# Last inverse transform of a spectral filter beside attention: constants as weights, the spectrum in two float32r parts as 256 moving columns, a turned output, and a new list of batches

## The chip, the cores and the metric

One core of a Trainium2 chip runs the whole kernel. Its engines are TensorE (PE, with the weight loads PEld), VectorE (DVE), ScalarE (ACT), GpSimd (POOL) and SyncE (SP, which issues most DMAs). The metric is the device time of one execution in microseconds; lower is better. The time before is the median of three runs.

## What is computed

Two independent layers read their own inputs; the results stand side by side in the last axis. The first is attention with 16 query heads of width 28 that share one key head and one value head, over 2048 rows. The second is a filter in the spectrum: a real two-dimensional Fourier transform over 2048 x 448, a product with complex weights, and the inverse transform.

```python
def _A_ref(x, wq, wk, wv, wo):
    q = (x @ wq).reshape(B, S, H, Dh).transpose(0, 2, 1, 3)
    k = x @ wk
    v = x @ wv
    scores = jnp.einsum("bhqd,bkd->bhqk", q, k) * (Dh ** -0.5)
    p = _softmax(scores, axis=-1)
    o = jnp.einsum("bhqk,bkd->bhqd", p, v)
    return o.transpose(0, 2, 1, 3).reshape(B, S, H * Dh) @ wo

def _B_ref(x, w_r, w_i):
    X = jnp.fft.rfft2(x, axes=(-2, -1))
    X = X * (w_r + 1j * w_i)
    return jnp.fft.irfft2(X, s=(S, D), axes=(-2, -1))
```

with B = 1, S = 2048, D = 448, H = 16, Dh = 28.

## The kernel before

**Attention.** After the projections (lines up to some 400) the work goes in 256 steps: 4 blocks of 512 queries (c) x 4 groups of 4 heads (g) x 16 blocks of 128 keys (kc). In a step PE makes four score tiles of 128 x 512 (line 867, float32r; here "a score"), ACT takes the exponential of each out of PSUM (line 811), and PE multiplies with the values (`flush`, line 822, four float32 products of 32 columns side by side). After 16 steps the sum of a (c, g) is turned (line 826) and normalised (`norm`, `divide`); the output projection is done in units of (c, k, g) (`wo_unit`, matmuls on line 731).

**The filter.** It is cut into matrix products, spread between the scores. Part one (`fft1_*`) transforms along D and partly along S, and writes `t1` to DRAM; it is nearly done before the 256 steps, and only the last unit, `fft1_b(7)`, stands among them. Part two (`fft2_a`, `fft2_b`, 16 units each) finishes the transform along S, multiplies with the weights, begins the inverse and writes `t2` to DRAM. Its operands are already kept as two float32r parts: a high part, which is a rounded copy, and a low part, which is the difference; `mm3` (line 555) adds three products: high by high, low by high, high by low. Part three reads `t2` back (`fft3_load`, eight loads q, each with its own constants `fi`):

- `fft3_a(q, e)` finishes the inverse along S for the even (e = 0) or odd (e = 1) frequencies of D: four float32 matmuls of 128 columns into one PSUM bank (line 655), and one DVE copy to `z` (line 658).
- `fft3_b(q, v)` does the inverse along D for 128 rows of the result: four float32 matmuls (line 669) in which a 128-column piece of `z` is the weights and the constants `cs3` are the 113 moving columns. DVE copies two of the products out (line 673), adds and subtracts (lines 674 and 675); POOL makes the final sums and differences (lines 679 and 680), and SP stores them (line 682).

**The list.** `PLAN` holds one string for each batch of steps; PE's order is written out by it. In a string, `-` is a score whose exponential ACT takes straight from PSUM; `k` is a score of the batch's last step that DVE copies to SBUF first (line 873) and ACT takes from there in one operation of 1024 columns (line 890); `e` is one of the last step that ACT takes at once. `F` is the last unit of part one, `A` and `B` a unit of `fft2_a` and `fft2_b`, `W` a unit of the output projection, `Z` a unit of part three in the order a, a, b, b for each q. X stands for WWWW and Y for ZZ. `spread(n, units, lazy, start, rest)` makes a string of n steps and sets the units at even distances: unit j at (4n - 4)(j + start)/(units + rest), less 0.4. The scores of a batch come first, its value products at the end; the last step's products wait for the next batch. `where` holds the step at which each unit falls, and with `at(step, ...)` loads and splits are hung on it: `fft3_load(q)` eight steps ahead of its first Z, but not before the last B.

**Banks and queues.** PSUM has eight banks. One holds the running sum of the value products; scores and units share the others through `take` and `give`, which choose the bank that a small model of the clocks of PE, ACT and DVE says is free first. A bank is free for PE again when the last operation that reads it is done. DVE, too, works in an order that is written out: what must follow a unit at once is put there, and other work (`put`) waits in two queues, from which `passed` takes operations as the modelled time goes on; `need(key)` takes them until the one named is out. SP and POOL issue DMAs in the order of the program and wait in it, so a transfer that waits holds up all behind it. `behind` sets an order of issue alone.

**Buffers.** The pool `fp` has tags that several tiles share, one after another: `wi` and `cst` hold `z` in part three, `pwr` holds `y1`, `pwi` holds `yo`, `cs` holds first `cs1` and later `cs3`, and `b2` holds the loaded `c2`.

Of the kernel before, what the change touches and what calls it, by code (L numbers as in the profile page):

```python
# [10 lines left out]
F32 = mybir.dt.float32  # L11
F32R = mybir.dt.float32r
# [3 lines left out]
ALU = mybir.AluOpType  # L16
AX = mybir.AxisListType
# [3 lines left out]
S, D, H = 2048, 448, 16  # L21
# [16 lines left out]
def spread(n, units, lazy=4, start=0.9, rest=0.85):  # L38

    m = 4 * n - 4  # L40
    out = [(float(i), "-") for i in range(m)]
    out += [(j + 0.5 if j < lazy else m + 0.1 * j, "k" if j < lazy else "e") for j in range(4)]
    out += [(m * (j + start) / (len(units) + rest) - 0.4, u) for j, u in enumerate(units)]
    return "".join(k for _, k in sorted(out)).replace("X", "WWWW").replace("Y", "ZZ")


PLAN = ["eeeeF", "eeee"] + 4 * [spread(2, "", 0)]
FIVE, SIX = spread(5, "BA"), {u: spread(6, u) for u in ("X", "Y", "BAX", "XBB")}
PLAN += [spread(5, "A", 4, 1.6), spread(5, "A")] + 11 * [FIVE] + [SIX["X"], FIVE, SIX["X"], SIX["BAX"], FIVE]
PLAN += [SIX["XBB"], spread(5, "")]  # L50
PLAN += 4 * [SIX["Y"]] + 4 * [SIX["X"]] + 7 * [SIX["Y"]] + 4 * [SIX["X"]] + 3 * [SIX["Y"]] + 2 * [spread(5, "Y")]


WARM = 10, 10
# [3 lines left out]
def kernel(ctx: ExitStack, tc: tile.TileContext, t: dict):  # L58
    nc = tc.nc
    mm = nc.tensor.matmul  # L60
# [3 lines left out]
    fp = ctx.enter_context(tc.tile_pool(name="fp", bufs=2))  # L64
# [29 lines left out]
    fc, xb, ff = {}, {}, {}  # L94
# [147 lines left out]
    with tc.tile_pool(name="w1", bufs=1) as w1:  # L242
# [37 lines left out]
        with tc.tile_pool(name="x1", bufs=2) as x1:  # L280
# [124 lines left out]
            for c in range(1, NC):  # L405
                for g in range(NG):
# [83 lines left out]
    d, f, a, b, e, c = free  # L490
# [34 lines left out]
    def passed(work):  # L525

        clock["pe"] += work
        while any(queue) and clock["dve"] <= clock["pe"]:
            pop()
        clock["dve"] = max(clock["dve"], clock["pe"] - 512)  # L530

    def at_once(work=640, engine="dve"):
        clock[engine] = max(clock[engine], clock["pe"] + 200) + work

    begun = []
# [41 lines left out]
    pr, cst = {}, {}  # L577
# [52 lines left out]


    def fft3_consts():
        fc["cs3"] = fp.tile([113, 4, 113], F32, name="cs3", tag="cs", bufs=1)
        behind(nc.gpsimd.dma_start(fc["cs3"], t["cs3"]), begun[-1])

    t2v = t2.rearrange("(r l n) h f -> r l h n f", r=2, l=2)
    c2 = {}
# [12 lines left out]
    def fft3_a(q, e):  # L650
        w, o0 = ((113, 0), (112, 113))[e]
        bank = take()
        pz = bank.rearrange("p (j n) -> p j n", j=4)
        for j in range(4):
            mm(pz[:w, j], c2["c", q][:, j, o0:o0 + w], c2["F", q][:, j], start=True, stop=True)  # L655
        passed(872)
        z = c2["z", q, e] = fp.tile([113, 2, 4, 64], F32, name=f"z{e}", tag=("wi", "cst")[e])
        nc.vector.tensor_copy(z[:w], pz[:w].rearrange("p j (r n) -> p r j n", r=2))
        at_once()
        give(bank)  # L660

    def fft3_b(q, v):
        ze, zo = c2["z", q, 0], c2["z", q, 1]
        cs3 = fc["cs3"]
        js = slice(2 * v, 2 * v + 2)
        bank = take()
        py = bank[:, :452].rearrange("p (k n) -> p k n", k=4)
        for k, (z, w, r) in enumerate(((ze, 113, 0), (zo, 112, 0), (zo, 112, 1), (ze, 113, 1))):
            mm(py[:, k], z[:w, r, js], cs3[:w, k], start=True, stop=True)  # L669
        passed(888)  # L670
        y1 = fp.tile([128, 2, 2, 113], F32, name="y1", tag="pwr")
        m = fp.tile([128, 2, 113], F32, name="m", tag="us", bufs=1)
        nc.vector.tensor_copy(m, py[:, 2:4])
        nc.vector.tensor_tensor(y1[:, :, 0], py[:, 0:2], m, op=ALU.add)
        nc.vector.tensor_tensor(y1[:, :, 1], py[:, 0:2], m, op=ALU.subtract)  # L675
        at_once(1100)
        give(bank)
        yo = fp.tile([128, 4, 113], F32, name="yo", tag="pwi")
        nc.gpsimd.tensor_tensor(yo[:, 0:2], y1[:, 0], y1[:, 1], op=ALU.add)  # L679
        nc.gpsimd.tensor_tensor(yo[:, 2:4], y1[:, 0], y1[:, 1], op=ALU.subtract)  # L680
        r0 = (2 * q + v) * 128
        nc.sync.dma_start(t["ob"][r0:r0 + 128], yo)


    oh, ol, osb = {}, {}, {}
# [76 lines left out]
    def at(step, f, *a):  # L762
        later.setdefault(max(step, 0), []).append((f, a))
# [3 lines left out]
            "B": [(fft2_b, u) for u in range(16)],  # L767
            "W": [(wo_unit, c, k, g) for c in range(NC - 1) for k in range(4) for g in range(NG)],
            "Z": [(f, q, e) for q in range(8) for f in (fft3_a, fft3_b) for e in range(2)]}
    todo = {k: deque(v) for k, v in todo.items()}  # L770

    where, total = {}, 0
    for tokens in PLAN:
        n, x = sum(k in "-ke" for k in tokens) // 4, 0
# [5 lines left out]
    fft2_consts()  # L780
    at(1, fft2_load, 0)
    at(where["A"][0] - 1, fft2_split, 0)
    at(14, fft3_consts)
    for u, step in enumerate(where["A"]):
        if u % 2 == 0 and u < 14:
            at(step - 1, fft2_load, u // 2 + 1)
# [59 lines left out]
    begin = 0  # L846
    for tokens in PLAN:
        n = sum(k in "-ke" for k in tokens) // 4
# [4 lines left out]
        new, lazy, x = [], [], {"-": 0, "k": 0}  # L853
        keep = [pp.tile([128, 2, CW], F32, name="k", bufs=4) for _ in range(2)]
        for k in tokens:
# [5 lines left out]
            i, h = divmod(x[kind], 4)  # L861
# [3 lines left out]
            c, g, kc = steps[i if kind == "-" else n - 1]  # L865
# [25 lines left out]
        else:  # L891
            for h in lazy:
                p = keep[h // 2][:, h % 2]
# [8 lines left out]
    c = NC - 1  # L902
# [30 lines left out]
    a, b, d = spare  # L933
    rv = nc.values_load(bits.bitcast(I32)[0:1, 0:1])
    with tc.If(rv > int(np.float32(BOUND).view(np.int32))), tc.tile_pool(name="g1", bufs=1) as g1:
# [12 lines left out]
        with tc.For_i(0, 64, 1) as n:  # L948
# [3 lines left out]
            for i in range(4):  # L952
                r = slice(32 * i, 32 * i + 32)
# [10 lines left out]
        w = g1.tile([128, NG, D], F32, name="w")  # L964
        nc.sync.dma_start(w, t["wo"][:, 0:NG])
        qv = qraw.rearrange("p g (c q) -> p c g q", q=CW)
        oa = t["oa"].rearrange("(n p) d -> n p d", p=128)
        with tc.For_i(0, NC, 1) as nq:
            y = g1.tile([128, 4, D], F32, name="y")
            nc.vector.memset(y, 0.0)  # L970
            with tc.For_i(0, NG, 1) as ng:
# [5 lines left out]
                for i in range(4):  # L977
                    r = slice(32 * i, 32 * i + 32)
                    acc = g1.tile([32, CW], F32, name="acc")
                    nc.vector.memset(acc, 0.0)  # L980
                    with tc.For_i(0, 16, 1) as nk:
# [5 lines left out]
                        p = g1.tile([128, CW], F32, name="pe")  # L987
# [3 lines left out]
                    z = g1.tile([32, CW], F32, name="z")  # L991
# [100 lines left out]
def _gather(oa, ob):  # L1092
    out = np.empty((1, S, 2 * D), np.float32)
    out[0, :, :D] = oa
    y = ob.reshape(32, 64, 4, 113).transpose(1, 0, 2, 3).reshape(S, 4, 113)
    d = np.arange(113)
    b = out[0, :, D:]
    b[:, d] = y[:, 0]
    b[:, D - d[1:]] = y[:, 1, 1:]
    b[:, D // 2 - d[:112]] = y[:, 2, :112]  # L1100
    b[:, D // 2 + d[1:112]] = y[:, 3, 1:112]
    return out


_OUTS = {"oa": (S, D), "ob": (S, 4, 113)}


# [14 lines left out]
```

## Time and profile before

| | before |
|---|---|
| median of 3 runs | 646.97 us (646.79 to 647.3) |
| profiled execution | 646.39 us, its span 644.5 us |
| ACT | 552.6 us busy, 86% |
| DVE | 370.6 us busy, 58% |
| POOL | 79.9 us busy, 12% |
| matmuls of fft3_a (line 655) | 128 instructions, first at 320.0 us, last at 611.3 us |
| matmuls of fft3_b (line 669) | 128 instructions, first at 333.0 us, last at 622.4 us |
| granted clock of PE | 0.999 |

The profile is of one execution. Times are in microseconds from the start of the span, "ns" where it says so. A row of the timeline gives the start, the length, engine, source line, operation, tiles written and read, shape, and how many equal instructions in a row were merged; in brackets stands idle time before it and what ended it. The length of merged matmuls runs to the modelled end of the last, so the pace of PE is read from start to start. A float32 matmul shows as two instructions, a float32r matmul as one. A row of grouped instructions gives the count, then busy time and the mean of one, then the idle time before them. In the rows of a line's own view, three figures with slashes are the shortest, median and longest duration in ns. A window's row has the busy times of PE, PEld, DVE, ACT and POOL in that order.

### The profile page before, as it was taken

To read this page: it belongs to the slowest core of one execution; us is meant where nothing else is said; L and a number is where in the kernel's file an instruction comes from. 1 tells how busy PE (TensorE), PEld (TensorE's weight loads), DVE (VectorE), ACT (ScalarE), POOL (GpSimd) and SP (SyncE) were. 2 spreads that over 40 slices of the span, in tenths; PEclk is the share of its full clock that TensorE was granted. 3 is DMA by queue.
4 is the path that set the end of the run, shared out by engine and by line. 5 is a ranking of instruction groups with operands and counts; after the bars stand their busy time and mean duration, and the time that the engine had idled before them with its cause. 6 is when DMAs were issued, how large, how long until landed. Compare 5 with 4: busy or idle time off the path is not lost.

```text
span 644.5 us, 12021 instructions
## 1 busy us (share of the span) xinstructions
PE 639.0 (99%) x4470; PEld 381.5 (59%) x4470; DVE 370.6 (58%) x683; ACT 552.6 (86%) x1011; POOL 79.9 (12%) x150
## 2 busy tenths in 40 slices
PE   9999999999999999999999999999999999999997
PEld 7877555555555556655555566556655566556655
DVE  5999538989997937465543523354545342363531
ACT  5655999999998989988999898998999898998891
POOL 3022301001211110001020300011031100010110
PEclk9999999999999999999999999999999999999999
DMA  8766953446734522213242403014241403131001
GB/s 275 263 182 167 269 135 101 115 99 155 189 87 112 142 59 72 55 59 103 56 114 59 114 16 80 29 41 122 52 122 42 103 15 80 44 92 20 30 31 60
DMA packets 36113, 63.83 MB, mean 99 GB/s; under 512 B 7905, under 2 KB 23922, under 8 KB 35084
## 3 DMA queue, kind: packets, MB, share of 16 engines
q1 hardware_dynamic: 30832, 49.60, 27.7%
q0 software_dynamic: 4640, 12.48, 7.5%
q10 hardware_dynamic: 576, 0.92, 0.4%
q8 instruction: 36, 0.59, 0.4%
q14 instruction: 29, 0.24, 0.1%
HBM read 30.04 MB, written 14.75 MB: 69 GB/s over the span
## 4 chain that ended last, share of the span: by engine, by line
PE 96%; DMA 1%; DVE 1%; SPq 1%; issue 0%; ACT 0%; ACTq 0%; DVEq 0%
PE s L867 30%; PE s L822 23%; PE po L822 7%; PE s L342 6%; PE sx L867 5%; PE sx L822 4%; PE po L867 4%; PE s L731 4%; PE s L140 2%; PE s L655 2%; PE s L669 2%; PE po L731 1%; PE pbb L159 1%; DMA qa<-qa 1%; PE s L290 1%; PE s L558 1%
## 5 line engine op out<-in xcount | busy, mean ns | idle before, releaser
L811 ACT ACTIVATE p<-s 128x512 f32<-128x512 f32 x632 | 340.1, 627 | 37.1 <-PE s L867 31.4
L867 PE MATMUL s<-qa,ka 128*128 128x512 f32 x782 | 238.0, 407 | 0.3 <-DMA qa<-qa 0.2
L867 PEld LDWEIGHTS s<-qa,ka 128*128 128x128 f32 x782 | 143.2, 188 | 73.7 <-issue 33.1
L873 DVE COPY k<-s 128x512 f32<-128x512 f32 x131 | 84.1, 683 | 125.4 <-PE s L867 125.4
L822 PE MATMUL s<-p,vs 128*32 128x512 f32 x1112 | 132.3, 595 | 0.0
L890 ACT ACTIVATE k<-k 128x1024 f32<-128x1024 f32 x88 | 90.3, 1108 | 0.0
L822 PEld LDWEIGHTS s<-p,vs 128*32 128x32 f32 x1112 | 33.5, 109 | 72.6 <-issue 70.9
L811 ACT ACTIVATE p<-sx 128x512 f32<-128x512 f32 x109 | 68.3, 626 | 7.0 <-PE sx L867 6.4
L811 ACT ACTIVATE p<-po 128x512 f32<-128x512 f32 x83 | 52.8, 636 | 4.8 <-PE po L867 2.3
L867 PE MATMUL sx<-qa,ka 128*128 128x512 f32 x130 | 53.2, 409 | 0.0
L867 PE MATMUL po<-qa,ka 128*128 128x512 f32 x112 | 45.2, 403 | 0.0
L822 PE MATMUL s<-k,vs 128*32 128x512 f32 x296 | 38.7, 594 | 0.0
L822 PE MATMUL po<-p,vs 128*32 128x512 f32 x328 | 38.5, 594 | 0.0
L695 POOL DMA_DIRECT2D ol<-ol x36 | 18.0, 508 | 130.1 <-DVE ol L718 65.4
L679 POOL TENSOR_TENSOR yo<-y 128x226 f32<-128x226 f32 x16 | 9.5, 596 | 190.7 <-DVE y L675 98.1
L867 PEld LDWEIGHTS sx<-qa,ka 128*128 128x128 f32 x130 | 24.4, 188 | 12.7 <-issue 5.0
L873 DVE COPY k<-po 128x512 f32<-128x512 f32 x27 | 18.5, 683 | 16.4 <-PE po L867 16.2
L867 PEld LDWEIGHTS po<-qa,ka 128*128 128x128 f32 x112 | 21.1, 188 | 7.6 <-issue 2.5
L822 PE MATMUL sx<-p,vs 128*32 128x512 f32 x208 | 24.8, 595 | 0.0
L826 DVE STREAM_TRANSPOSE osb<-s 128x512 f32<-128x512 f32 x11 | 7.9, 716 | 29.2 <-PE s L822 29.2
L822 PEld LDWEIGHTS po<-p,vs 128*32 128x32 f32 x328 | 9.8, 110 | 21.9 <-issue 21.3
L342 PE MATMUL s<-xh,wqh 128*128 128x512 f32 x56 | 22.7, 404 | 0.0
(224 smaller groups left out, 780.6 us busy)
## 6 DMA issues: line engine op xcount, KB each, us to landing
qa<-qa SPq DMA_DIRECT2D x15, 512.0 KB
raw<-xa SPq DMA_DIRECT2D x16, 256.0 KB
xb<-xb SPq DMA_DIRECT2D x8, 512.0 KB
qa<-qh SPq DMA_DIRECT2D x64, 64.0 KB
qa<-ql SPq DMA_DIRECT2D x60, 64.0 KB
ob<-yo SPq DMA_DIRECT2D x16, 226.0 KB
t<-bs SPq DMA_DIRECT2D x16, 225.0 KB
wr<-wr POOLq DMA_DIRECT2D x16, 225.0 KB, 4.6
```

The costliest lines, as they stand in the source:

```text
L140: mm(pa[r0:r0 + 32, e, o0:o0 + n], f[:, 2 * r + k, 2 * p + e, h], cs1[:, 2 * r + k, :n], start=True, stop=True)
L342: mm(pq, w[:, j, gs], x[:, j], start=(j == 0 and n == 0), stop=(j == 3 and n == 1))
L655: mm(pz[:w, j], c2["c", q][:, j, o0:o0 + w], c2["F", q][:, j], start=True, stop=True)
L669: mm(py[:, k], z[:w, r, js], cs3[:w, k], start=True, stop=True)
L679: nc.gpsimd.tensor_tensor(yo[:, 0:2], y1[:, 0], y1[:, 1], op=ALU.add)
L695: nc.gpsimd.dma_start(ol[c][o, g].bitcast(F32), ol[c][r, 0].bitcast(F32))
L731: mm(p, x[c][:, g, s], w, start=(g == 0 and n == 0), stop=(g == NG - 1 and n == 2))
L811: nc.scalar.activation(tiles[-1][:, h % 2], sc, AF.Exp, scale=SCALE)
L822: mm(po[c, g][32 * i:32 * i + 32], vs[:, kc], ps[i // 2][:, i % 2], start=(n == 1), stop=(n == 16))
L867: begun.append(mm(sc, ka[:, kc * 128:(kc + 1) * 128], qa[c, g][:, h], start=True, stop=True))
L873: nc.vector.tensor_copy(keep[h // 2][:, h % 2], sc)
L890: nc.scalar.activation(p, p, AF.Exp, scale=SCALE)
```

## The change

The constants `cs3` become weights, in a high and a low float32r part; they are loaded and split after the last B, not at step 14. `fft3_a` keeps `z` as a high and a low part: one more DVE operation that reads PSUM, with the odd high part in the space of the tile `c2` that the matmuls have just read. In `fft3_b`, v now names a pair of products (k = v and v + 2) and no longer 128 rows: each product is three float32r matmuls with 256 moving columns, and the result lies turned, 113 points of D on the partitions and 256 rows in the columns. The sums and differences within the pair are made at once on DVE with 256 columns; after v = 1 the final difference and sum over both units are two DVE operations of 512 columns from the queue, each with its store. The host's reordering of `ob` follows the new layout. The list is written anew: F moves from the first batch to the second, most batches with A and B have both units one score later, and the batches of W, A, B and Z stand in another order.

```diff
-PLAN = ["eeeeF", "eeee"] + 4 * [spread(2, "", 0)]
-FIVE, SIX = spread(5, "BA"), {u: spread(6, u) for u in ("X", "Y", "BAX", "XBB")}
-PLAN += [spread(5, "A", 4, 1.6), spread(5, "A")] + 11 * [FIVE] + [SIX["X"], FIVE, SIX["X"], SIX["BAX"], FIVE]
-PLAN += [SIX["XBB"], spread(5, "")]
-PLAN += 4 * [SIX["Y"]] + 4 * [SIX["X"]] + 7 * [SIX["Y"]] + 4 * [SIX["X"]] + 3 * [SIX["Y"]] + 2 * [spread(5, "Y")]
+PLAN = ["eeee"] + ["eeeeF"] + [spread(2, "", 0, 1.05)] + 3 * [spread(2, "", 0)] + [spread(5, "A", 4, 1.6)]
+PLAN += [spread(5, "BA", 4, 0.9, 0.6)] + [spread(5, "A")] + 6 * [spread(5, "BA", 4, 0.9, 0.6)]
+PLAN += [spread(5, "BA", 4, 0.75, 0.6)] + 3 * [spread(5, "BA", 4, 0.9, 0.6)] + [spread(6, "X", 4, 0.9, 0.6)]
+PLAN += [spread(6, "X")] + [spread(5, "BAB", 4, 0.9, 0.6)] + [spread(6, "AX")]
+PLAN += [spread(5, "BAB", 4, 0.9, 0.6)] + [spread(6, "BX")] + [spread(6, "Y")] + [spread(5, "")]
+PLAN += 2 * [spread(6, "Y")] + [spread(6, "Y", 4, 0.9, 0.6)] + [spread(6, "X", 4, 0.9, 0.6)]
+PLAN += [spread(6, "X", 4, 0.9, 0.73)] + [spread(6, "X")] + [spread(6, "Y")] + [spread(6, "X", 4, 0.9, 0.6)]
+PLAN += 6 * [spread(6, "Y")] + 2 * [spread(6, "X")] + [spread(6, "X", 4, 0.9, 0.73)] + [spread(6, "Y")]
+PLAN += [spread(6, "X")] + [spread(5, "Y", 4, 1.2)] + [spread(6, "Y")] + [spread(5, "Y", 4, 1.2)]
+PLAN += [spread(6, "Y")]
...
     def fft3_consts():
-        fc["cs3"] = fp.tile([113, 4, 113], F32, name="cs3", tag="cs", bufs=1)
-        behind(nc.gpsimd.dma_start(fc["cs3"], t["cs3"]), begun[-1])
+        c = fp.tile([113, 4, 113], F32, name="cs3", tag="wi")
+        behind(nc.gpsimd.dma_start(c, t["cs3"]), begun[-1])
+        h = fc["cs3h"] = fp.tile([113, 4, 113], F32R, name="cs3h", tag="cs", bufs=1)
+        l = fc["cs3l"] = fp.tile([113, 4, 113], F32R, name="cs3l", tag="bh", bufs=1)
+        put("cs3", [(400, lambda: nc.vector.tensor_copy(h, c)),
+                    (630, lambda: nc.vector.tensor_tensor(l, c, h.bitcast(F32), op=ALU.subtract))])
...
-        z = c2["z", q, e] = fp.tile([113, 2, 4, 64], F32, name=f"z{e}", tag=("wi", "cst")[e])
-        nc.vector.tensor_copy(z[:w], pz[:w].rearrange("p j (r n) -> p r j n", r=2))
-        at_once()
+        if e:
+            h = c2["c", q].rearrange("p j f -> p (j f)")[:113, :512].bitcast(F32R)
+            h = h.rearrange("p (r j n) -> p r j n", r=2, j=4)
+        else:
+            h = fp.tile([113, 2, 4, 64], F32R, name="zh", tag="wi")
+        l = fp.tile([113, 2, 4, 64], F32R, name="zl", tag=("cst", "ph")[e])
+        c2["z", q, e] = h, l
+        z = pz[:w].rearrange("p j (r n) -> p r j n", r=2)
+        nc.vector.tensor_copy(h[:w], z)
+        nc.vector.tensor_tensor(l[:w], z, h[:w].bitcast(F32), op=ALU.subtract)
+        at_once(1330)
         give(bank)
 
     def fft3_b(q, v):
...
+        need("cs3")
         bank = take()
-        py = bank[:, :452].rearrange("p (k n) -> p k n", k=4)
-        for k, (z, w, r) in enumerate(((ze, 113, 0), (zo, 112, 0), (zo, 112, 1), (ze, 113, 1))):
-            mm(py[:, k], z[:w, r, js], cs3[:w, k], start=True, stop=True)
-        passed(888)
-        y1 = fp.tile([128, 2, 2, 113], F32, name="y1", tag="pwr")
-        m = fp.tile([128, 2, 113], F32, name="m", tag="us", bufs=1)
-        nc.vector.tensor_copy(m, py[:, 2:4])
-        nc.vector.tensor_tensor(y1[:, :, 0], py[:, 0:2], m, op=ALU.add)
-        nc.vector.tensor_tensor(y1[:, :, 1], py[:, 0:2], m, op=ALU.subtract)
+        py = bank[:113].rearrange("p (k n) -> p k n", k=2)
+        for i, k in enumerate((v, v + 2)):
+            e = k in (1, 2)
+            w, r = (112 if e else 113), k // 2
+            h, l = (x[:w, r].rearrange("p j n -> p (j n)") for x in c2["z", q, e])
+            a, b = fc["cs3h"][:w, k], fc["cs3l"][:w, k]
+            mm(py[:, i], a, h, start=True, stop=False)
+            mm(py[:, i], b, h, start=False, stop=False)
+            mm(py[:, i], a, l, start=False, stop=True)
+        passed(730)
+        x = c2["y", v] = fp.tile([113, 2, 256], F32, name="y1", tag=("pwr", "pl")[v])
+        m = fp.tile([113, 256], F32, name="m", tag="us", bufs=1)
+        nc.vector.tensor_copy(m, py[:, 1])
+        nc.vector.tensor_tensor(x[:, 0], py[:, 0], m, op=ALU.add)
+        nc.vector.tensor_tensor(x[:, 1], py[:, 0], m, op=ALU.subtract)
         at_once(1100)
         give(bank)
-        yo = fp.tile([128, 4, 113], F32, name="yo", tag="pwi")
-        nc.gpsimd.tensor_tensor(yo[:, 0:2], y1[:, 0], y1[:, 1], op=ALU.add)
-        nc.gpsimd.tensor_tensor(yo[:, 2:4], y1[:, 0], y1[:, 1], op=ALU.subtract)
-        r0 = (2 * q + v) * 128
-        nc.sync.dma_start(t["ob"][r0:r0 + 128], yo)
+        if v:
+            x0, d = c2["y", 0], fp.tile([113, 2, 256], F32, name="yo", tag="pwi")
+
+            def total():
+                nc.vector.tensor_tensor(x, x0, x, op=ALU.add)
+                nc.sync.dma_start(t["ob"][q, 0], x)
+
+            def difference():
+                nc.vector.tensor_tensor(d, x0, x, op=ALU.subtract)
+                nc.sync.dma_start(t["ob"][q, 1], d)
+
+            put(("y", q), [(600, difference), (600, total)], True)
...
-    at(14, fft3_consts)
+    at(where["B"][-1] + 1, fft3_consts)
```

More of the change, by code (lines that the diff above doesn't have):

```diff
@@ L660, in fft3_a @@
+        c2["z", q, e] = h, l
[3 more added lines that the diff above has]
+        at_once(1330)
         give(bank)
     def fft3_b(q, v):
-        ze, zo = c2["z", q, 0], c2["z", q, 1]
-        cs3 = fc["cs3"]
-        js = slice(2 * v, 2 * v + 2)
+        need("cs3")
         bank = take()
-        py = bank[:, :452].rearrange("p (k n) -> p k n", k=4)
-        for k, (z, w, r) in enumerate(((ze, 113, 0), (zo, 112, 0), (zo, 112, 1), (ze, 113, 1))):
-            mm(py[:, k], z[:w, r, js], cs3[:w, k], start=True, stop=True)
@@ L1094, in _gather @@
     out[0, :, :D] = oa
-    y = ob.reshape(32, 64, 4, 113).transpose(1, 0, 2, 3).reshape(S, 4, 113)
+    y = ob.reshape(8, 2, 113, 2, 4, 64).transpose(5, 0, 4, 1, 3, 2).reshape(S, 4, 113)
     d = np.arange(113)
@@ L1102, in _gather @@
     return out
-_OUTS = {"oa": (S, D), "ob": (S, 4, 113)}
+_OUTS = {"oa": (S, D), "ob": (8, 2, 113, 2, 256)}
 def kernel(**inputs):
```

## The prediction

> **What bounds the kernel now.** I read the page first: the busy shares, then the chain of waits.
>
> ```profile
> span 644.5 us, 12021 instructions
> PE 639.0 (99%) x4470; PEld 381.5 (59%) x4470; DVE 370.6 (58%) x683; ACT 552.6 (86%) x1011; POOL 79.9 (12%) x150
> PE 96%; DMA 1%; DVE 1%; SPq 1%; issue 0%; ACT 0%; ACTq 0%; DVEq 0%
> ```
>
> TensorE (PE) sets the end almost alone, so a nanosecond taken from its stream is a nanosecond of the kernel, unless a wait grows in its place. The modelled ends of matmuls hide short waits; these are read from the starts in the timeline. A batch of the list begins where scores (L867) follow the value products (L822). Here is PE in one six-step batch with the third part's second half (L669), and Vector (DVE) beside it, in two answers of the timeline.
>
> ```profile
> 567.56 0.50 PE L867 MATMUL sx<-qa,ka 128*128 128x512 f32 x1
> 567.90 1.56 PE L867 MATMUL s<-qa,ka 128*128 128x512 f32 x6
> 569.30 0.40 PE L867 MATMUL sx<-qa,ka 128*128 128x512 f32 x1
> 569.53 1.56 PE L867 MATMUL s<-qa,ka 128*128 128x512 f32 x6
> 570.92 1.04 PE L669 MATMUL s<-cs,z 113*128 113x113 f32 x8
> 572.63 2.65 PE L867 MATMUL s<-qa,ka 128*128 128x512 f32 x9
> 575.12 0.40 PE L867 MATMUL sx<-qa,ka 128*128 128x512 f32 x1
> ...
> 580.73 0.73 PE L867 MATMUL s<-qa,ka 128*128 128x512 f32 x2
> ```
>
> ```profile
> 572.41 0.39 DVE L673 COPY m<-s 128x226 f32<-128x226 f32 x1
> ...
> 573.70 0.40 DVE L673 COPY m<-sx 128x226 f32<-128x226 f32 x1
> ```
>
> Thirteen scores take 3.02 us (567.90 to 570.92), 232 ns each. After L669 nine take 2.49 us (572.63 to 575.12), 0.40 us more than 9 x 0.232; for most of it PE waits for PSUM banks that ScalarE (ACT) and DVE have yet to empty. The batch lasts 13.17 us (567.56 to 580.73). How slowly scores start behind float32 work alone, and how a row of scores ends, shows behind a pair of fft3_a:
>
> ```profile
> 611.33 0.47 PE L867 MATMUL po<-qa,ka 128*128 128x512 f32 x1
> ...
> 613.04 0.40 PE L867 MATMUL s<-qa,ka 128*128 128x512 f32 x1
> 613.37 1.06 PE L822 MATMUL s<-p,vs 128*32 128x512 f32 x8
> ```
>
> From 611.33 to 613.04 seven scores take 1.71 us where 1.62 is due: 0.09 us for the start, and no wait besides.
>
> **The matmuls of fft3_b.** Before, a unit (one q and v) has four float32 matmuls, two instructions each. The two units of a batch are 16 instructions in 1.71 us (570.92 to 572.63), 107 ns each; with the slow start of 0.09 a pair is 1.80 us. After, a unit has six float32r matmuls of 256 columns, 12 to a pair, one instruction each as the 1,024 score matmuls are. No row shows float32r at 256 columns. The nearest is the output projection with 448:
>
> ```profile
> 385.44 0.36 PE L731 MATMUL s<-woh,oh 128*128 128x448 f32 x1
> ...
> 387.47 0.37 PE L731 MATMUL s<-wol,oh 128*128 128x448 f32 x1
> ```
>
> Ten of these take 2.03 us, 203 ns each. In proportion to the score's 512, 256 columns are 116 ns; with a fixed 14 ns and 0.425 ns a column, which fits 203 and 232 about as well, 123. I take 120. From below the weights bound it: L669 loads new weights every 107 ns. From above, 232, if half the columns saved nothing. So a pair costs 12 x 0.120 = 1.44 us (1.28 to 2.78) in place of 1.80, and there is no change of kind any more, so no slow start. Eight pairs: **-2.9 us** (-4.2 to +7.8).
>
> This needs each weight load to be hidden behind the matmul before it. What an open load costs is seen at the start of a batch: 567.56 to 567.90 is 0.34 us, 0.11 over a score. What speaks for hiding is the load's own row:
>
> ```profile
> L669 PEld LDWEIGHTS s<-cs,z x88: 186/192/193, 332.9 to 621.4; 113*128 113x128 f32 x44, 112*128 112x128 f32 x44
> ```
>
> A load lasts 192 ns while L669's instructions follow each other every 107, all on the same rows of the array: loads run beside matmuls. The Trainium skill, "TensorE: Matmul & The Clock Gate", Part 3, "The mechanism", has it that a load overlaps matmuls in flight only where its row group differs. With the same page's columns/1.2 under "LDWEIGHTS" (an estimate of 94 ns for 113) that rule would make a pair 12 x 0.214 = 2.57 us and the kernel slower. The 107 ns beside 192 speaks against it here; it is weighed as a rival.
>
> **What is given back behind the pair.** It is 0.36 us shorter, so the scores behind it start earlier, but the two y banks are not free that much earlier: DVE takes 1.29 us a unit (572.41 to 573.70), and with 256 in place of 226 columns 1.29 to 1.46 in proportion. ACT frees a bank per 0.478 us (five starts in 2.39 us, 114.06 to 116.45, below), which no edit changes. So part of the 0.36 turns into the bank wait that is already there. Bounds: 0, and 8 x 0.36 = 2.9. But in the last such batch ACT itself stood waiting for a score:
>
> ```profile
> 622.91 1.09 ACT L811 ACTIVATE p<-s 128x512 f32<-128x512 f32 x2 [0.49 <-PE s L867]
> ```
>
> Where it stands, it moves up with the scores; I take a third, **+1.0 us**.
>
> **The first half, fft3_a, and the sums.** Its matmuls stay. Each unit adds a subtraction out of PSUM before its bank is free, and the final sums move from POOL to DVE. The nearest subtraction with a float32r result:
>
> ```profile
> L208 DVE TENSOR_TENSOR ql<-ql,qh 128x512 fp32r<-128x512 f32 x16 | 11.2, 702 | 0.2
> ```
>
> Sixteen subtractions and sixteen sums of 0.70 us are 22 us more on a DVE that is busy 371 of 644 us (58%). The hold is what matters: with two such operations more in its row the second z bank returns up to 1.4 us later, and the first score that lacks a bank waits. Bounds: nothing, or 1.4 us in eight batches, 11 us. In that time ACT frees three banks and PE asks for six. The scores at 611.33 wait for none, so some are spare; I take **+0.3 us**. POOL loses 32 sums; it is 12% busy and has no share of the chain: 0. The stores of the result (16, each of the same size as before) wait on SP for DVE, not for POOL, and hold up the loads queued behind them, which fetch what is due eight steps later: 0.
>
> **The list.** Counting its letters, both lists hold the same 50 batches (26 of six steps, 18 of five, 4 of two, 2 of one) and the same units, so only waits can change. The final unit of part one moves four scores later: 0, the same work in another order, its reader (the first A) some ten steps away; bounds 0.9 us either way, the four scores. In ten of the five-step batches with B and A both units stand one score later. Such a batch with its wait, and one that has none:
>
> ```profile
> 109.85 0.97 PE L867 MATMUL s<-qa,ka 128*128 128x512 f32 x3
> ...
> 120.56 0.73 PE L867 MATMUL s<-qa,ka 128*128 128x512 f32 x2
> ```
>
> ```profile
> 206.59 0.97 PE L867 MATMUL s<-qa,ka 128*128 128x512 f32 x3
> ...
> 217.08 0.50 PE L867 MATMUL s<-qa,ka 128*128 128x512 f32 x1
> ```
>
> ```profile
> 111.89 1.11 ACT L811 ACTIVATE p<-s 128x512 f32<-128x512 f32 x2
> 113.09 0.60 ACT L811 ACTIVATE p<-po 128x512 f32<-128x512 f32 x1
> ...
> 114.06 2.57 ACT L811 ACTIVATE p<-s 128x512 f32<-128x512 f32 x5
> 116.45 0.67 ACT L811 ACTIVATE p<-sx 128x512 f32<-128x512 f32 x1
> ```
>
> The first lasts 10.71 us, the second 10.49: 0.22 of wait. ACT starts two in 1.20 us (111.89 to 113.09), 0.24 idle, for want of scores during the unit of B. With one score more ahead of that unit ACT has this work, and frees its banks earlier. Ten batches could gain 2.2 us, or wait as long again at the score put ahead; I take **-1.5 us**. The batches of steps 75 to 119 are recombined from W, BA, BAX, XBB to W, BAB, AX, BX with the same units: bounds 0.4 either way (two such waits), taken as 0. The constants' load moves from step 14 to behind the last B: one DMA on POOL ahead of the first c loads, and two DVE operations (a copy and a subtraction, at most 1.4 us) that no unit needs for 15 steps: 0; without that cover, 1.4 us and the landing. The last B is at step 104 and the first third-part unit at 111, seven steps where there were ten (106 and 116):
>
> ```profile
> 306.89 2.84 SPq L646 DMA_DIRECT2D c<-t  x6
> 320.04 1.95 PE L655 MATMUL s<-fi,c 128*113 128x128 f32 x16
> ```
>
> The c loads end their issue at 309.73, 10.3 us ahead of their reader. Three steps fewer, at 10.71/5 = 2.1 us each, leave 3.9: 0.
>
> **The sum.** -2.9 +1.0 +0.3 -1.5 = -3.1 us. The profiled execution took 646.39 us (span 644.5 and 1.9 around it), 0.58 under the median of 646.97; 646.39 - 3.1 = 643.3, and against the median **643.9 us**.
>
> **Rivals.** (1) Waits take the place: the 2.9 us return whole behind the pairs, and the list gives half of its 1.5: with 0.3 for z, 646.5. For it: the batch at 567.56 already waits behind its pair; against: ACT's idle 0.49. (2) Loads stay open: 0.11 us on each of 96 matmuls, 10.6 us; -3.1 + 10.6 = +7.5, 654.5. The change loses as soon as a matmul takes over 1.80/12 = 150 ns. For it: the load at a batch's start is open; against: L669's pitch. (3) DVE binds: the second z bank, 1.4 us late, holds up scores once fewer than two others are spare; at half of it in eight batches, 5.6 in place of 0.3, +2.2, 649.2. For it: DVE works in order, with whole operations of 0.7 us ahead; against: 42% of it is free. (4) The list gives all of its 2.2 and waits go elsewhere too (0.8): 642.4.
>
> **How the numbers follow.** Forecast 0.60, rival (4) 0.10, (1) 0.13, (2) 0.07, (3) 0.10. No change means within 0.2%, 1.3 us, of 646.97. Forecast and (4) are faster, but for 0.02 at the forecast's edge: faster 0.68; (1) and that edge: same 0.15; (2) and (3): slower 0.17. The forecast's own range is 642.4 to 645.5. The range for 8 in 10 takes in (4) and (1): 641.6 to 647.6, which leaves out (2), (3) and little else.
>
> **What would show it.** Twelve float32r matmuls of 256 columns a pair, 1.4 to 1.5 us from the first start to the next score; if 2.5, rival (2). Six-step batches with them about 12.7 us, not 13.17; if unchanged with a longer row of scores behind the pair, (1). If batches with the first half grow by over 0.3 us, (3). Batches with B and A at 10.5, not 10.71. It is wrong altogether if the gain sits before step 10, or if the time falls by over 5 us.

## The result and the profile after

| | before | after |
|---|---|---|
| median | 646.97 us | 673.42 us (672.54 to 673.76) |
| ratio, 95% interval | | 1.0405 [1.0391, 1.0419] |
| profiled execution | 646.39 us, span 644.5 | 673.42 us, span 671.6 |
| granted clock of PE, mean | 0.999 | 0.979 |

The kernel became 26 us slower; 643.9 us had been predicted, with 647.6 as the upper end. The page of after, with its chain of waits:

```profile
span 671.6 us, 11945 instructions
...
PE 639.2 (95%) x4438; PEld 379.5 (57%) x4438; DVE 394.5 (59%) x717; ACT 550.3 (82%) x1011; POOL 61.2 (9%) x118
...
PE   9999999999999999999999299999999499999995
...
PEclk9999999999999999999999699999999889999998
...
PE 86%; DMA 9%; SPq 1%; DVE 1%; ACT 1%; issue 0%; ACTq 0%; DVEq 0%
```

PE is as busy as before (639.2 and 639.0 us), but in a span 27 us longer. The slices show that nothing became slower throughout: one slice falls to 2, one to 4 and the last to 5 (it was 7 before), and everything else is full. The granted clock falls in the same slices. In the chain 9% of the span now belongs to DMA. The waits of PE name the transfers (microseconds in total, how often, the longest):

```profile
PE s L759 <- DMA oh<-ol: 13.1, 1, 13.1
PE s L895 <- DMA qa<-qa: 9.7, 1, 9.7
```

Two single waits, one of an output projection for its turned heads (`oh`), one of the scores for their queries (`qa`). Neither transfer belongs to the part that was changed. The timeline of PE shows the first wait, and that of SP what stood in the queue ahead of it:

```profile
370.82 0.36 PE L759 MATMUL s<-wol,oh 128*128 128x448 f32 x1
384.29 0.71 PE L759 MATMUL s<-woh,oh 128*128 128x448 f32 x1 [13.11 <-DMA oh<-ol]
```

```profile
360.72 0.26 SPq L708 DMA_DIRECT2D ob<-yo  x1
361.20 2.47 SPq L220 DMA_DIRECT2D qa<-qa  x1
363.73 0.53 SPq L704 DMA_DIRECT2D ob<-y  x1
364.30 12.70 SPq L720 DMA_DIRECT2D oh<-ol  x4
```

Two stores of the result (L708 and L704) are issued, and then four small `oh` transfers need 12.70 us for their issue alone. The windows of after say what the DMA engines do meanwhile; the last two columns are the share of the core's 16 engines that is busy, and GB/s:

```profile
335.20:347.00 11.80, 11.80 (x83) 7.08 (x76) 5.15 (x8) 10.85 (x21) 0.00 (x0) 1.00 0.06 23
372.00:378.00 6.00, 0.00 (x0) 0.00 (x0) 0.00 (x0) 0.00 (x0) 0.00 (x0) 0.65 0.07 29
```

A share of 0.06 is one engine of sixteen. In the first window only a pair of stores is under way, and PE does not need what is behind it; in the second, PE, ACT, DVE and POOL all stand still, and again one engine moves all there is. In the trace a store of after is 113 packets of 2,048 bytes, one for each row and each 0.084 us long, which follow one another on one engine: some 9.5 us a store and 19 us the pair, longer where other packets come between. Before, the tile had 128 rows. Both kernels' DMA tables list 16 stores of 226 KB each: the bytes are equal, the rows are not, and 113 is prime.

The packets also show what a later transfer waits for. The `qa` transfer at 361.20 is issued between the two stores and has 64 packets of 8,192 bytes. Sixty of them start from 364.3 to 367.5 us; the last four, one sixteenth, run from 372.78 to 374.01, just between the end of the first store's packets (372.78) and the start of the second's (374.01). So the part of this transfer that falls to the store's engine waits until the store is through, and the rest does not.

What it costs, by the lengths of batches from start to start, against the same kernel with its stores cut (e1 below): the batch at 365.83 lasts 28.07 us in place of 13.24, the one at 525.50 lasts 25.85 in place of 13.42, and from the last batch's start to the end of the span it is 32.21 in place of 28.36. That is 14.8 + 12.4 + 3.9 = 31.1 of the 32.1 us between the two spans; the other microsecond lies ahead of the first score, which starts at 69.98 in after and at 68.93 in e1. The 3.9 us at the end are the last pair of stores: ACT's last activation starts 24.5 us behind the start of the last batch in both kernels, but in after the pair's packets run on until 669.4. The second stall follows two pairs of stores, as the chain of waits has it (start, length, what):

```profile
483.34 20.35 DMA ob<-y
507.56 21.60 DMA ob<-y
531.28 4.39 DMA qa<-qa
```

It lasts longer than its 9.71 us of waiting, as the scores behind it show:

```profile
535.71 2.50 PE L895 MATMUL s<-qa,ka 128*128 128x512 f32 x5 [9.71 <-DMA qa<-qa]
538.00 0.63 PE L895 MATMUL po<-qa,ka 128*128 128x512 f32 x1
538.43 2.33 PE L895 MATMUL s<-qa,ka 128*128 128x512 f32 x5
540.57 0.63 PE L895 MATMUL po<-qa,ka 128*128 128x512 f32 x1
540.99 0.46 PE L895 MATMUL s<-qa,ka 128*128 128x512 f32 x1
```

Twelve scores from 535.71 to 540.99 take 5.28 us where 12 x 0.232 = 2.78 is due: in this stretch the granted clock is 0.50, and a stall is paid once more in the work behind it.

### The profile page after: what moved, and what is told of

Same layout as the page of the kernel before. It is cut to its first block, busy times and chain, and to the rows that moved or that the text cites. A ratio compares the mean times of both kernels' runs of the same rounds, so it can differ in the third digit from the quotient of the medians.

```text
span 671.6 us, 11945 instructions
## 1 busy us (share of the span) xinstructions
PE 639.2 (95%) x4438; PEld 379.5 (57%) x4438; DVE 394.5 (59%) x717; ACT 550.3 (82%) x1011; POOL 61.2 (9%) x118
## 4 chain that ended last, share of the span: by engine, by line
PE 86%; DMA 9%; SPq 1%; DVE 1%; ACT 1%; issue 0%; ACTq 0%; DVEq 0%
PE s L895 27%; PE s L850 21%; DMA ob<-y 6%; PE s L347 5%; PE sx L850 5%; PE po L850 4%; PE po L895 4%; PE sx L895 4%; PE s L759 4%; PE s L145 2%; PE s L664 1%; DMA oh<-ol 1%; SPq L720 1%; PE pbb L164 1%; DMA raw<-wq 1%; PE s L562 1%
## 5 line engine op out<-in xcount | busy, mean ns | idle before, releaser
L895 PEld LDWEIGHTS s<-qa,ka 128*128 128x128 f32 x785 | 145.5, 190 | 81.9 <-issue 28.5
L839 ACT ACTIVATE p<-po 128x512 f32<-128x512 f32 x95 | 60.8, 640 | 7.4 <-PE po L895 6.6
L839 ACT ACTIVATE p<-sx 128x512 f32<-128x512 f32 x96 | 61.5, 641 | 5.2 <-PE sx L895 3.9
L895 PE MATMUL po<-qa,ka 128*128 128x512 f32 x121 | 49.7, 411 | 0.0
L895 PE MATMUL sx<-qa,ka 128*128 128x512 f32 x118 | 47.7, 405 | 0.0
L850 PE MATMUL sx<-p,vs 128*32 128x512 f32 x320 | 38.2, 595 | 0.0
L759 PE MATMUL s<-woh,oh 128*128 128x448 f32 x46 | 17.6, 382 | 13.1 <-DMA oh<-ol 13.1
L901 DVE COPY k<-po 128x512 f32<-128x512 f32 x24 | 16.4, 681 | 21.2 <-PE po L895 21.2
L766 DVE COPY ya<-s 128x448 f32<-128x448 f32 x10 | 6.2, 625 | 36.8 <-PE s L759 30.0
L850 PE MATMUL po<-p,vs 128*32 128x512 f32 x208 | 24.8, 595 | 0.0
```

Of the source, the lines that this page charges most:

```text
L759: mm(p, x[c][:, g, s], w, start=(g == 0 and n == 0), stop=(g == NG - 1 and n == 2))
L839: nc.scalar.activation(tiles[-1][:, h % 2], sc, AF.Exp, scale=SCALE)
L850: mm(po[c, g][32 * i:32 * i + 32], vs[:, kc], ps[i // 2][:, i % 2], start=(n == 1), stop=(n == 16))
L895: begun.append(mm(sc, ka[:, kc * 128:(kc + 1) * 128], qa[c, g][:, h], start=True, stop=True))
L901: nc.vector.tensor_copy(keep[h // 2][:, h % 2], sc)
```

## The experiments

The theory to be tested was: a store of 113 rows from SP uses one DMA engine, everything issued later that has a share on that engine waits, and the rest of the change is worth what the prediction gave it. Against it stood: that stores of the new layout are slow whatever their rows, that DVE issues them too late, that SP is the bottleneck, and that the new list puts stores and readers too close together. Ratios are to the kernel before on the same chip; its median is 647.40 us for e1, e2, e3 and e5, 646.95 for e4, e6 and e7, and 646.90 for e8 to e10. Medians from different chips are compared below by what each lies under its own before.

| run | median us | ratio, 95% interval |
|---|---|---|
| e1_store112 | 643.01 | 0.9934 [0.9918, 0.9951] |
| e2_pad120 | 642.69 | 0.9921 [0.9903, 0.9938] |
| e6_store_pool | 642.29 | 0.9932 [0.9915, 0.9948] |
| e7_cuts | 642.32 (one execution) | |
| e4_before_113rows | 679.37 | 1.0520 [1.0488, 1.0551] |
| e3_list_only | 642.90 | 0.9932 [0.9915, 0.9948] |
| e5_third_only | 647.61 | 1.0005 [0.9995, 1.0014] |
| e8_z_first | 641.05 | 0.9909 [0.9894, 0.9924] |
| e9_b_defer | 641.48 | 0.9915 [0.9902, 0.9929] |
| e10_both | 639.70 | 0.9889 [0.9873, 0.9904] |

**e1: after, each store cut in two, 112 rows and one row.**

```diff
-                nc.sync.dma_start(t["ob"][q, 0], x)
+                nc.sync.dma_start(t["ob"][q, 0, :112], x[:112])
+                nc.sync.dma_start(t["ob"][q, 0, 112:], x[112:])
```

The same for the difference, one edit of two lines.

> The changed kernel with each of its 16 result stores cut into rows 0 to 111 and row 112; nothing else differs. Theory (a store of 113 rows goes through one DMA engine and holds up what SP has queued behind it): the 226 packets of 2 KB that took some 19 us one after another spread over 16 engines, a store lands in under 5 us, the two long batches (28.07 and 25.85 us) return to about 13.3, and the time is 641 to 645 us. Rival (Vector holds the banks, or the list brings the loads too late): the long batches stay and the time is over 660 us.

Measured: 643.01 us. SP's timeline in the same place:

```profile
359.67 0.34 SPq L709 DMA_DIRECT2D ob<-yo  x1
...
360.79 0.43 SPq L710 DMA_DIRECT2D ob<-yo  x1
361.27 0.32 SPq L704 DMA_DIRECT2D ob<-y  x1
361.63 1.90 SPq L705 DMA_DIRECT2D ob<-y  x1
363.58 2.70 SPq L722 DMA_DIRECT2D oh<-ol  x4
```

```profile
359.00:367.00 8.00, 8.00 (x60) 3.42 (x60) 4.53 (x8) 6.82 (x13) 2.53 (x5) 1.00 0.71 176
```

The four `oh` transfers are issued in 2.70 us and no longer 12.70; the DMA share in this window is 0.71. Of PE's waits nothing is left but 1.1 us at the start. The bytes, the layout, the list, SP's queue and DVE's part are those of after: what differs is the count of rows in a transfer. The Trainium skill, "DMA: Bandwidth & Descriptors", "Why a DMA increments its semaphore by 16 and not by 1", says that the number of engines of a transfer is the largest number up to 16 that divides the slowest dimension of both its sides. By that rule 113 rows get one engine and 112 rows sixteen; the shares 0.06 and 0.71 agree.

**e2: after, the constants padded with zeros to 120 columns**, so that products, sums and stores have 120 rows; seven rows of the output hold nothing and the host drops them.

```diff
-        h = fc["cs3h"] = fp.tile([113, 4, 113], F32R, name="cs3h", tag="cs", bufs=1)
+        h = fc["cs3h"] = fp.tile([113, 4, 120], F32R, name="cs3h", tag="cs", bufs=1)
...
-        x = c2["y", v] = fp.tile([113, 2, 256], F32, name="y1", tag=("pwr", "pl")[v])
+        x = c2["y", v] = fp.tile([120, 2, 256], F32, name="y1", tag=("pwr", "pl")[v])
```

> The changed kernel with the constants padded to 120 columns by zeros, so that products, sums and stores have 120 rows (seven of them unused) and no store is cut. Theory (one engine, because 113 rows do not divide): 120 rows divide by 15, the store spreads over 15 engines, 641 to 645 us, within 0.3% of the kernel with cut stores. Rival (Vector, banks or list): over 660 us.

Measured: 642.69 us, with more bytes (240 KB a store) and no cut.

**e6: after, the uncut stores, both of a pair, issued by POOL in place of SP.**

```diff
-                nc.sync.dma_start(t["ob"][q, 0], x)
+                nc.gpsimd.dma_start(t["ob"][q, 0], x)
```

> The changed kernel with its 113-row stores issued by POOL in place of SP. Theory (the software queue spreads 113 rows over the engines, as its 113-row load of cs3 landed in 3.2 us, and nothing stands behind them): 641 to 645 us. Rival (113 rows go through one engine from any queue, and hold up the transfers of both): over 655 us.

Measured: 642.29 us, without waits of PE. The table of DMA issues gives the median time to landing last:

```profile
ob<-yo POOLq DMA_DIRECT2D x8, 226.0 KB, 2.7
ob<-y POOLq DMA_DIRECT2D x8, 226.0 KB, 3.5
```

So the 113 rows are no obstacle in themselves: from POOL's queue they land in 2.7 and 3.5 us, where a store takes about 9.5 from SP. The same section of the Trainium skill has an exception for some copies issued from GpSimd, which get 16 engines though their rows do not divide so; these rows agree with it.

**e7: after, the stores of each q cut at another row**: whole, 112 + 1, 110 + 3, 104 + 9, 96 + 17, 88 + 25, 64 + 49, 112 + 1.

```diff
+            def store(i, y):
+                cut = (113, 112, 110, 104, 96, 88, 64, 112)[q]
+                for r in (slice(0, cut), slice(cut, 113)):
+                    if r.start < 113:
+                        nc.sync.dma_start(t["ob"][q, i, r], y[r])
```

> The changed kernel with a store cut otherwise in each q, for the packets alone: 113 rows whole (q = 0), 112+1, 110+3, 104+9, 96+17, 88+25, 64+49, 112+1. Theory (as many engines as the largest divisor of the row count up to 16): the main pieces go through 1, 16, 11, 13, 16, 11, 16, 16 engines, the rests through 1, 3, 9, 1, 5, 7, 1; at 0.084 us a packet and two packets a row the first takes 19 us, 112 rows 1.2, 110 rows 1.7, 17 rows on one engine 2.9. Rival (only a multiple of 16 rows spreads, all else goes through one engine): 110, 104 and 88 rows take 15 to 18 us.

The number of packets in that expectation is wrong: a store has 113 packets of 2,048 bytes, one a row, and 226 are the pair. Measured in the packets of the trace, for the pair of a q:

| q and cut | 226 packets in us | packets in flight, mean |
|---|---|---|
| 0: 113 | 21.0 | about 1 |
| 2: 110 + 3 | 3.18 | 7.5 |
| 5: 88 + 25 | 2.97 | 8.3 |
| 6: 64 + 49 | 3.07 | 9.1 |
| 7: 112 + 1 | 2.12 for 223 of them, 3.39 for all | 11.3 in the 2.12 |

In q 1 (112 + 1) and q 3 (104 + 9) a `qa` transfer is issued among the pieces and breaks the row of packets; there the pair takes a little over 5 us. In q 4 (96 + 17) loads with packets of the same size follow too closely to be told apart. The whole store again moves one packet after another, though no stall follows it here. Cuts at 110, 104 and 88 rows spread too, where the rival had 15 to 18 us, so it isn't a matter of multiples of 16. The largest divisor up to 16 (11 for 110 and for 88 rows, 16 for 64 and 112) stands above every mean in the table, as it must; the trace doesn't name the engine of a packet, so the exact number of engines isn't shown.

**e4: before, with its stores of 128 rows cut into 113 and 15.** If the theory holds, the fault can be put into the kernel before, where nothing else of the change is present.

```diff
-        nc.sync.dma_start(t["ob"][r0:r0 + 128], yo)
+        nc.sync.dma_start(t["ob"][r0:r0 + 113], yo[:113])
+        nc.sync.dma_start(t["ob"][r0 + 113:r0 + 128], yo[113:])
```

> The kernel before with each of its 16 result stores (128 rows of 1808 B) cut into 113 and 15 rows, nothing else. Theory (113 rows go through one DMA engine): 113 packets one after another at some 0.08 us, 9 us for a store that took about 2, and with two in a batch some 18 us of one engine; transfers behind them on SP wait, so the kernel before becomes slower, 648 to 660 us. Rival (the new stores are slow because of their 4 KB rows or their new place): 646.5 to 648 us.

Measured: 679.37 us, 32 us slower than before and well beyond the 648 to 660 expected. The waits of PE:

```profile
PE po L732 <- DMA oh<-ol: 11.6, 1, 11.6
PE s L868 <- DMA oh<-ol: 7.7, 1, 7.7
```

The second wait holds up a score, which reads `qa`, though the profile names `oh`. The two long stalls come where they come in after, in the first batch of output projections behind a run of fft3 batches; two shorter ones, of 2.6 and 3.2 us, come ahead of the first scores of two fft3_b batches. The four batches that start at 368.65, 474.69, 513.71 and 580.73 in before last 26.84, 15.60, 23.55 and 16.10 us in place of 13.43, 12.88, 13.43 and 12.89, 29.5 us together; the last batch with what follows it adds 2.9. The direction was right and the size a miss: I had counted with one or two stalls of a few microseconds. How long a stall lasts hangs on what lies behind the store and when it is due, not on the store's own time, which is much the same as in after (a packet starts 0.075 us behind the one before it, at the median, and 0.080 in after). (The rows of the new stores have 2 KB, not the 4 KB that the expectation names.)

**e3: before, with the new list alone; e5: the third part alone** (e1, with the old list).

> The kernel before with the new list of batches alone; its third part, its stores and the place of its constants' load as before. Theory (the list is a gain of some 3 to 4 us, read from the starts of the batches up to step 120): 643 to 644.5 us. Rival (the list is what delays the queue's transfers): over 655 us, with the same long batches.

> The changed kernel with stores cut at row 112 and the old list of batches. Theory (what the pair of fft3_b saves, 0.36 us, is given back by banks that DVE holds longer in both halves): 646 to 648 us. Rival (the third part gains what its matmuls save): 644 to 645.5 us. Rival (the third part itself is the loss): over 655 us.

Measured: the list alone gives 642.90 us, a little below the 643 to 644.5 expected, 4.1 under the median of before and 4.5 under that of its own chip; the third part alone, freed of its stores, gives 647.61 us, no change. Batches by start to start (before, list only): the twelve five-step batches behind the first with an A 128.46 and 126.52 us, the six with output projections, A and B 78.67 and 77.29, from there to the end 338.06 and 336.65. For the third part the batches with fft3_a and with fft3_b have to be read apart; q is the order in which they come, the last batches of the list left out:

| | fft3_a, us | fft3_b, us |
|---|---|---|
| list only | 12.88 12.88 12.88 12.88 12.88 13.12 | 12.94 13.07 13.00 13.17 13.00 13.00 13.01 |
| after | 13.09 13.10 13.11 13.09 13.09 13.37 | 12.85 13.07 12.86 13.07 12.91 12.87 12.86 |

Each of these fft3_a batches loses 0.2 us, 1.3 together (the two of five steps that are left out last 11.03 and 11.21 us with the list only, 11.01 and 11.21 in after), and the fft3_b batches gain 0.7 together where each has 0.36 us less of work. The pair itself, in the timeline of after:

```profile
450.45 0.28 PE L688 MATMUL s<-zh,cs3h 113*113 113x256 f32 x1
...
451.76 0.28 PE L690 MATMUL s<-zl,cs3h 113*113 113x256 f32 x1
451.88 0.40 PE L895 MATMUL s<-qa,ka 128*128 128x512 f32 x1
452.11 0.40 PE L895 MATMUL po<-qa,ka 128*128 128x512 f32 x1
452.35 1.41 PE L895 MATMUL s<-qa,ka 128*128 128x512 f32 x5
453.75 0.50 PE L895 MATMUL po<-qa,ka 128*128 128x512 f32 x1
```

Twelve matmuls from 450.45 to 451.88, 1.43 us, 119 ns each; the scores follow without a slow start (0.23 from 451.88 to 452.11), and five take 1.40 (452.35 to 453.75) where 1.16 is due: 0.24 us of waiting for a bank (in the trace the score at 453.75 is released by an exponential of ACT). Two edits to e2 were made to free the two kinds of bank earlier.

**e8: `z` is copied out of PSUM in one operation**, and its high and low parts are made from SBUF, out of the queue. **e9: the y bank is free after two operations**: the copy goes into `y1` itself, the sum reads PSUM, and the difference is made from SBUF as the sum less twice the copy. **e10: both.**

```diff
-        nc.vector.tensor_copy(h[:w], z)
-        nc.vector.tensor_tensor(l[:w], z, h[:w].bitcast(F32), op=ALU.subtract)
-        at_once(1330)
+        zf = fp.tile([113, 2, 4, 64], F32, name="zf", tag="pwi")[:w]
+        nc.vector.tensor_copy(zf, z)
+        at_once()
...
+        put(("z", q, e), [
+            (430, lambda: nc.vector.tensor_copy(h[:w], zf)),
+            (690, lambda: nc.vector.tensor_tensor(l[:w], zf, h[:w].bitcast(F32), op=ALU.subtract))], True)
```

```diff
-        nc.vector.tensor_copy(m, py[:, 1])
-        nc.vector.tensor_tensor(x[:, 0], py[:, 0], m, op=ALU.add)
-        nc.vector.tensor_tensor(x[:, 1], py[:, 0], m, op=ALU.subtract)
-        at_once(1100)
+        nc.vector.tensor_copy(x[:, 1], py[:, 1])
+        nc.vector.tensor_tensor(x[:, 0], py[:, 0], x[:, 1], op=ALU.add)
+        at_once(800)
...
+            put(("m", q, v), [(420, lambda: nc.vector.scalar_tensor_tensor(
+                x[:, 1], x[:, 1], -2.0, x[:, 0], op0=ALU.mult, op1=ALU.add))], True)
```

> The kernel padded to 120 rows, with fft3_a copying z out of PSUM as float32 first, which frees the bank after one operation as before; the high and the low part are then made from SBUF, out of the queue (one more DVE operation a unit). Theory (the batches with the first half are 0.2 us longer because the bank is held through the subtraction): these batches go from 13.09 to 12.9 us, 1.2 to 1.8 us in all, 641 to 641.8 us beside 642.7. Rival (they are longer because DVE has more to do): 642.5 to 644 us.

> The kernel padded to 120 rows, with fft3_b freeing its bank after two operations: the copy goes into y1 itself, the sum reads PSUM, and the difference is made from SBUF out of the queue as the sum less twice the copy. Theory (the rest of the 0.36 us that a pair saves is lost to y banks that come back late): the batches with the second half go from 12.9 to about 12.7 us, 0.8 to 1.6 us in all, 641.2 to 642. Rival (ACT, not the y banks, sets the pace there): 642.4 to 643.2 us.

> Both of these edits together. Theory: the gains add, 639.8 to 641 us, so the third part then gives 2 to 3 us beside the list's 4. Rival (ACT and Vector give no more): 642 to 643.5 us.

Measured: 641.05, 641.48 and 639.70 us, where e2 has 642.69. The row of scores behind fft3_a, in the timeline of after and then of e8:

```profile
464.97 0.47 PE L895 MATMUL s<-qa,ka 128*128 128x512 f32 x1
...
466.65 0.46 PE L895 MATMUL po<-qa,ka 128*128 128x512 f32 x1
467.11 0.74 PE L895 MATMUL s<-qa,ka 128*128 128x512 f32 x2
467.77 1.07 PE L850 MATMUL sx<-p,vs 128*32 128x512 f32 x8
```

```profile
449.64 0.93 PE L899 MATMUL s<-qa,ka 128*128 128x512 f32 x3
450.41 0.40 PE L899 MATMUL sx<-qa,ka 128*128 128x512 f32 x1
450.64 1.64 PE L899 MATMUL s<-qa,ka 128*128 128x512 f32 x6
452.21 1.06 PE L854 MATMUL po<-p,vs 128*32 128x512 f32 x8
```

Ten scores take 2.80 us in after and 2.57 in e8. From the score at 466.65 to the next it is 0.46 us. The trace has that next score, at 467.11, released by an exponential of ACT that ends at 467.07; DVE's second subtraction, and with it the second z bank, ends only at 467.18. So PE has to wait for a bank of ACT's while DVE still holds the z bank, and that wait is gone in e8. Its fft3_a batches last 12.85 to 12.90 us, but for the sixth with 13.12, where e2 has 13.08 to 13.13 and 13.36, and so are as long as with the list alone; its fft3_b batches are unchanged. In e9 the fft3_b batches that had 13.07 and 13.08 come to 12.84, the fft3_a batches stay; the 12.7 expected is not reached. The batches hold 0.7 of the 1.2 us between the medians of e9 and e2, and the other 0.5 lies between the chips: e2 is 4.7 us under its own before, e9 5.4, e8 5.9 and e10 7.2. So e8 gains 1.1 on e2, e9 0.7 and e10 2.5. e10, with 639.70 us, is faster than both kernels, and 2.7 us beyond the list alone (4.5), which is what the third part is worth when its stores and its banks are in order. In its fft3_b batches, 12.84 and 12.85 us but for one with 12.90, a wait is left at the end of the scores:

```profile
436.89 0.42 PE L899 MATMUL s<-qa,ka 128*128 128x512 f32 x1
437.30 0.51 PE L899 MATMUL po<-qa,ka 128*128 128x512 f32 x1
```

It is 0.41 from one score to the next where 0.23 is due. In the trace an exponential of ACT, from 436.51 to 437.25, releases that score, so the rival of e9, that ACT sets the pace there, holds for what is left.

## Why the prediction was wrong

**The failed step** is the last sentence of the part on fft3_a and the sums: "The stores of the result (16, each of the same size as before) wait on SP for DVE, not for POOL, and hold up the loads queued behind them, which fetch what is due eight steps later: 0." The size is the same, the shape isn't: 128 rows became 113. It named as queued behind the stores only the loads of part three; `qa` and `oh`, on the same queue, are due far sooner, and the stall came at them. The step cost some 31 us. e1, e2 and e6 take it away in three unlike ways and land within 0.8 us of each other; e4 puts it into the kernel before. None of the four rivals held it: all looked for the loss on PE and DVE.

**The matmuls of fft3_b** were right: 1.43 us a pair beside 1.44, 119 ns each beside 120. Rival (2), loads that stay open, falls; so does, for this case, the Trainium skill's rule weighed there, that a load hides only beside another row group, which would have made it 2.57.

**The give-back behind the pair** was undersized: of 2.9 us I kept 1.9, and the seven batches that can be compared gained 0.7, the tail 0.2 (28.5 in the list alone, 28.4 in e1). So about 2 us went back into bank waits, close to rival (1)'s course for this term. e9 shows that part of it hung on the bank's third DVE operation.

**fft3_a** was given +0.3 and cost 1.3 us with the new list; with the old one, where the batches of e5 last 13.10 to 13.42 and those of before 12.88 to 13.17, the seven full ones and the short one cost 2.3. The mechanism is rival (3)'s, the z bank held through the subtraction, at 0.2 to 0.5 a batch and not its 0.7. The row I argued from, scores that wait for nothing behind fft3_a, showed one batch without a spare bank being needed; it didn't show that one was left over. e8 settles it.

**The list** was given -1.5 and gave 4.1 to 4.5. The batches with B and A went as described, here with their score more ahead of the unit of B, in the timeline of after:

```profile
100.20 0.97 PE L895 MATMUL s<-qa,ka 128*128 128x512 f32 x3
...
110.72 0.51 PE L895 MATMUL s<-qa,ka 128*128 128x512 f32 x1
```

10.52 us, not 10.71; the twelve batches gained 1.9 together. Mis-sized was the rest: the recombination of W, A and B, taken as 0 with bounds of 0.4, gave 1.4, and the later half, with four of its eight batches of output projections one score later, another 1.4. What made these two terms wasn't taken apart, and the score ahead of the unit is only part of it. Of the first 1.4, 0.8 lies in the first batch of output projections (14.14 us before, 13.31 with the new list), which before also waited for its queries:

```profile
228.50 0.47 PE L867 MATMUL s<-qa,ka 128*128 128x512 f32 x1 [0.20 <-DMA qa<-qa]
```

Of the second 1.4, the eight batches of output projections hold 0.5, the seven of fft3_b 0.3 and the first six of fft3_a 0.6, though the units of most of these stand where they stood.

Without the stores the terms measured are -0.9 for fft3_b, +1.3 for fft3_a and about -4.3 for the list, -3.9 in place of -3.1; e1's 643.01 and e6's 642.29 lie inside the predicted range. So a forecast of 643.9 came out near what the kernel does without a fault that the forecast had looked at and passed over. Even there luck has a part: fft3_b and fft3_a came out 1.0 worse each and the list 2.8 better, and these errors cancel but for 0.8.

## What to carry to other kernels

Where a change turns a tile, compare the rows of its transfers, not their bytes: here 113 rows, which no number from 2 to 16 divides, put a whole store from SP on one DMA engine (a share of 0.06), and the price was paid by transfers of `oh` and `qa`, far from the change in the code. Padding to 120 rows, cutting off the odd row, or issuing from POOL each took it away here for the cost of a line. And where a bank is held by several operations in a row, the first copy out of PSUM should free it, and the rest be made from SBUF; that was worth 2.5 us in e10, beside e2.

## What the runs showed of the hardware that was not expected

- A store of 113 rows of 2,048 bytes from SP runs on one engine at 0.084 us a row, some 24 GB/s, and holds not only packets but issues: four later `oh` transfers took 12.70 us on SP beside 2.70. From POOL the same store lands in 2.7 to 3.5 us.
- A wait costs more than its length. In the first stall the granted clock of PE (the column ahead of the DMA share) falls to 0.50 and is 0.83 on average in the 9.6 us behind it; behind the second, scores take 0.43 us, not 0.23, for some 5 us (the timeline at 535.71 above). The windows of after:

```profile
378.00:384.30 6.30, 0.01 (x1) 0.04 (x1) 0.00 (x0) 0.00 (x0) 0.00 (x0) 0.50 0.26 77
384.30:393.90 9.60, 9.60 (x60) 4.79 (x60) 0.63 (x1) 6.50 (x11) 0.00 (x0) 0.83 0.07 26
```

- Float32r matmuls of 256 columns, each with new weights of 113 columns, follow each other every 119 ns, while a load lasts some 175 ns: the loads stay hidden.
- The start of the first score differs by up to 1.7 us between profiles, with either list (69.0 to 70.0 us with the old, 68.9 to 70.6 with the new), so that spans of single profiles are worse than batch lengths for differences of this size.
